# Four interleaved layers on one core: the TensorE program written out as a list of tokens, with pieces of layers 0, 1 and 2 in another order

## The chip, the cores and the metric

The kernel runs on one core of a Trainium2 chip. The time is the device time of one execution in microseconds (us); the kernel before has a median of 444.94 us over 13 runs (441.31 to 448.36). The profile shows one execution of its own, of 445.72 us. Engines are named as in the profile: PE is TensorE (PEld its weight loads), DVE VectorE, ACT ScalarE, POOL GpSimd, SP SyncE, which here only issues DMAs.

## The reference

One sequence of 2048 tokens by 512 features passes through four residual layers: a linear-attention block (A), a gated feed-forward block (B), and the same two with the same weights again. The listing is cut to what is computed.

```python
def _A_ref(x, wqkv, wo):                      # 32 heads of 16
    q, k, v = ...                             # from x @ wqkv
    phi = lambda t: jnp.where(t > 0, t + 1, jnp.exp(t)) + 1e-6
    pq, pk = phi(q), phi(k)
    kv = jnp.einsum("bhsd,bhse->bhde", pk, v)
    z = jnp.einsum("bhsd->bhd", pk)
    num = jnp.einsum("bhqd,bhde->bhqe", pq, kv)
    den = jnp.einsum("bhqd,bhd->bhq", pq, z)[..., None] + 1e-6
    return (num / den) ... @ wo
def _B_ref(x, w_gate, w_up, w_down):          # inner size 1792
    return (silu(x @ w_gate) * (x @ w_up)) @ w_down

x = x + _A_ref(_layernorm(x), A_wqkv, A_wo)   # layer 0
x = x + _B_ref(_layernorm(x), ...)            # layer 1
x = x + _A_ref(_layernorm(x), A_wqkv, A_wo)   # layer 2
x = x + _B_ref(_layernorm(x), ...)            # layer 3
```

The sums kv and z run over all 2048 tokens, so no token's attention output exists before the last key is in.

## The kernel before

**Tiles.** The tokens are 16 tiles of 128 (`T`), in 4 groups of 4 (`G`, `TG`). X, all weights and the normalised X of an attention layer (`xnA`) stay in SBUF. The 512 features are 4 chunks of 128 (`NC`), the inner size is 14 chunks (`NF`).

**Steps.** A layer's input is normalised by tile in `ln`: mean and variance (layer 0: DVE; later layers: a row sum that the residual addition leaves in `sums`, then an ACT Square with a sum), 1/sqrt on POOL (L462), then normalised on DVE (L473), or in layer 0 for 12 tiles on ACT (L469) with a factor from POOL (L466). A DMA issued on SP then transposes the tile into `xnT` (L489); only the first four tiles of layer 0 go through PE instead (L481). An attention layer then has these steps:

- `k_proj` and `q_proj`: 4 matmuls each, 128x512. `phi` follows: an exponential on ACT (L502), on about half of them an addition on ACT (L505), and minimum and maximum on DVE (L507, L511 or L514).
- `g_acc`: G = xn^T pk, summed over 16 tiles in four pinned PSUM banks; `z_acc`: the sums of keys, four 128x1 matmuls per tile.
- `z_fin`, `g_copy`, `kvt`, `m_mm`: the masked z, the copies of G, then kv and its product with Wo, which ends as `GT`.
- `den`: 16 matmuls of 128x8 give the denominators of a group of queries; DVE adds 1e-6 and takes the reciprocal (L608, L611), ACT spreads it over 16 columns (`rrep`, L616, four per group), SP issues a DMA that transposes each into `RT` (L620), and DVE multiplies the queries by it (L626).
- `wo`: 4 matmuls per tile, then DVE adds the residual (L637) and `ln` of the next layer starts for this tile.

A feed-forward layer has `gu` (gate and up of one chunk for one group: 8 matmuls, tanh on ACT L656, two DVE operations L658 and L661) and `dn` (one tile's output: 14 matmuls, residual on DVE L677).

**Order.** The order of PE's instructions is the order in which Python issues them. For the other engines `schedule` takes among the instructions that could start soonest the one whose result is due first by its own estimates; after that each engine runs its list strictly in order, and `sync` adds a semaphore wait wherever an operand comes from another engine. On PE, in layer 0, the products `gz` run two tiles behind the keys and queries of groups 0 and 1 are mixed in from tile 10. After the last `gz` come `z_fin`, `g_copy`, `den` of group 0, and so on; `wo` of groups 0 and 1 stand before the first `gu`; `weave` spreads the eight `wo` of groups 2 and 3 over the first two groups of layer 1. The keys of layer 2 for tiles 0 to 11 are mixed into layer 1's groups 1 to 3; G, z and the queries of layer 2 follow after layer 1 has ended. In layer 2 the list holds 15 of the 16 projections of queries: the first one of group 2 is in the `else` branch, which layer 2 doesn't take, and isn't issued.

**Weights.** The keys' weights come on ACT's queue at the start, X on SP's. The other weights are issued on POOL's queue, first the queries' weights (`Wq`), then the rest, in pairs tied to the keys of tile 7 and later (`load_next`).

The pieces meet in these lines of the main program:

```python
q(0, 1, 3)
gz(0, T - 1)
for L in (0, 2):
    z_fin(L)
    g_copy()
```

## Time and profile before

| what | value |
| --- | --- |
| median of 13 runs (lowest, highest) | 444.94 us (441.31, 448.36) |
| the profiled execution: its time, its span | 445.72 us, 444.0 us |
| busy in the span: PE, DVE, ACT, POOL | 420.3, 301.3, 189.9, 65.0 us |
| mean granted PE clock | 0.988 |
| DMA traffic | 24.28 MB, of which 16.27 MB on SP's queue (with the transposes) |

A row of the trace's list in order of time has the start, the time until the last of its instructions ended, the engine and the line, then the operation, its tiles and shape, the count, and in brackets how long the engine had been idle and whose result it then had. Matmuls overlap: a run of them is read from its start to the start of the next run. All `mm` calls have the one line L366, so matmuls are told apart by tiles: `pb<-pk,xnA` is G, `pb<-ones,pk` is z, `pb<-Wqkv,xnT` a key, `pb<-xnT,Wqkv` a query, `pb<-Zm,pq` a den, `pb<-GT,Wqkv` kv, `pb<-GT,pq` a `wo`, `pb<-xnT,Wg` and `pb<-xnT,Wu` gate and up, `pb<-Wd,hT` a `dn`.

### The profile page before, as it was taken

To read this page: it belongs to the slowest core of one execution; us is meant where nothing else is said; L and a number is where in the kernel's file an instruction comes from. 1 tells how busy PE (TensorE), PEld (TensorE's weight loads), DVE (VectorE), ACT (ScalarE), POOL (GpSimd) and SP (SyncE) were. 2 spreads that over 40 slices of the span, in tenths; PEclk is the share of its full clock that TensorE was granted. 3 is DMA by queue.
4 is the path that set the end of the run, shared out by engine and by line. 5 is a ranking of instruction groups with operands and counts; after the bars stand their busy time and mean duration, and the time that the engine had idled before them with its cause. 6 is when DMAs were issued, how large, how long until landed. Compare 5 with 4: busy or idle time off the path is not lost.

```text
span 444.0 us, 6441 instructions
## 1 busy us (share of the span) xinstructions
PE 420.3 (95%) x2135; PEld 192.7 (43%) x2177; DVE 301.3 (68%) x653; ACT 189.9 (43%) x361; POOL 65.0 (15%) x167
## 2 busy tenths in 40 slices
PE   6969986999999999999999997799999999999997
PEld 2434432444444444444444452344444444444443
DVE  6936878886698568738853278988758846854761
ACT  4953678444345334424432158754413402311320
POOL 4853202221211020020002000321100100000000
PEclk9999999999999999999999998999999999999999
DMA  7499543322312020011001002441130020001001
GB/s 236 78 170 337 199 96 71 60 38 47 61 36 25 3 44 1 1 25 24 1 1 38 12 1 59 84 83 37 37 83 13 13 49 24 0 13 35 1 1 47
DMA packets 56721, 24.28 MB, mean 55 GB/s; under 512 B 50736, under 2 KB 55344, under 8 KB 56688
## 3 DMA queue, kind: packets, MB, share of 16 engines
q1 hardware_dynamic: 54560, 16.27, 18.0%
q0 software_dynamic: 1584, 7.08, 4.9%
q10 hardware_dynamic: 544, 0.52, 0.4%
q8 instruction: 17, 0.28, 0.3%
q14 instruction: 16, 0.13, 0.1%
HBM read 9.70 MB, written 2.10 MB: 27 GB/s over the span
## 4 chain that ended last, share of the span: by engine, by line
PE 80%; DVE 7%; DMA 4%; POOL 3%; ACT 2%; issue 2%; SPq 1%; DVEq 0%; ACTq 0%
PE pb L366 80%; POOL rstd L462 1%; DMA Wqkv<-in_A_wqkv_dram 1%; DVE X L637 1%; SPq L620 1%; DMA xnT<-xnB 1%; DMA RT<-rrep 1%; DVE stats L445 1%; DVE pq L514 1%; ACT rrep L616 1%; DVE etmp L507 1%; DMA X<-in_A_x_dram 1%; POOL vpe L447 1%; POOL nmr L466 0%; DVE tht L658 0%
## 5 line engine op out<-in xcount | busy, mean ns | idle before, releaser
L656 ACT ACTIVATE tht<-pb 128x512 f32<-128x512 f32 x112 | 66.8, 596 | 131.1 <-PE pb L366 127.2
L366 PE MATMUL pb<-xnT,Wg 128*128 128x512 bf16 x439 | 114.9, 381 | 6.2 <-DMA xnT<-xnB 5.7
L366 PE MATMUL pb<-xnT,Wu 128*128 128x512 bf16 x438 | 114.4, 381 | 0.5
L366 PE MATMUL pb<-Wd,hT 128*128 128x512 bf16 x438 | 97.1, 379 | 0.5
L658 DVE SCALAR_TENSOR_TENSOR tht<-tht,pb 128x512 f32<-128x512 f32 x112 | 76.8, 686 | 22.6 <-ACT tht L656 19.4
L661 DVE TENSOR_TENSOR hT<-tht,pb 128x512 bf16<-128x512 f32 x112 | 76.9, 686 | 10.3 <-PE pb L366 0.5
L366 PEld LDWEIGHTS pb<-xnT,Wg 128*128 128x128 bf16 x448 | 43.9, 98 | 58.8 <-issue 6.6
L366 PEld LDWEIGHTS pb<-xnT,Wu 128*128 128x128 bf16 x448 | 44.0, 98 | 53.5 <-issue 0.9
L366 PEld LDWEIGHTS pb<-Wd,hT 128*128 128x128 bf16 x448 | 43.7, 98 | 52.4
L502 ACT ACTIVATE etmp<-pb 128x512 bf16<-128x512 f32 x63 | 37.4, 597 | 47.3 <-PE pb L366 45.5
L458 POOL TENSOR_SCALAR vpe<-mv 128x1 f32<-128x1 f32 x48 | 10.0, 209 | 266.9 <-ACT xnB L455 158.5
L366 PE MATMUL pb<-GT,pq 128*128 128x512 bf16 x127 | 33.3, 396 | 4.7 <-DVE pq L626 4.3
L462 POOL TENSOR_TENSOR rstd<-vpe,negh 128x1 f32<-128x1 f32 x64 | 36.7, 574 | 6.3
L366 PE MATMUL pb<-xnT,Wqkv 128*128 128x512 bf16 x118 | 30.1, 382 | 3.7 <-DMA Wqkv<-in_A_wqkv_dram 3.3
L507 DVE TENSOR_SCALAR etmp<-etmp 128x512 bf16<-128x512 bf16 x63 | 18.2, 291 | 22.2 <-ACT etmp L502 21.3
L366 PE MATMUL pb<-Wqkv,xnT 128*128 128x512 bf16 x123 | 32.7, 384 | 0.5 <-issue 0.2
L366 PE MATMUL pb<-pk,xnA 128*128 128x512 bf16 x127 | 32.7, 383 | 0.1
L677 DVE SCALAR_TENSOR_TENSOR pq<-pb,X 128x512 bf16<-128x512 f32 x16 | 11.1, 692 | 30.7 <-PE pb L366 30.7
L455 ACT ACTIVATE xnB<-X,mv 128x512 bf16<-128x512 bf16 x32 | 23.0, 721 | 11.7 <-DVE mv L452 10.5
L473 DVE TENSOR_SCALAR xnA<-X,mv,rstd 128x512 bf16<-128x512 bf16 x20 | 8.2, 411 | 26.1 <-POOL rstd L462 26.1
L455 ACT ACTIVATE xnA<-X,mv 128x512 bf16<-128x512 bf16 x16 | 11.5, 722 | 33.4 <-DVE mv L452 33.4
L637 DVE SCALAR_TENSOR_TENSOR X<-pb,X 128x512 bf16<-128x512 f32 x32 | 21.9, 683 | 1.9 <-PE pb L366 1.9
(62 smaller groups left out, 284.8 us busy)
## 6 DMA issues: line engine op xcount, KB each, us to landing
out_dram<-pq SPq DMA_DIRECT2D x16, 128.0 KB, 1.7
Wu<-in_B_w_up_dram POOLq DMA_DIRECT2D x4, 448.0 KB, 6.0
Wg<-in_B_w_gate_dram POOLq DMA_DIRECT2D x4, 448.0 KB, 6.4
X<-in_A_x_dram SPq DMA_DIRECT2D x6, 256.0 KB, 5.3
Wd<-in_B_w_down_dram POOLq DMA_DIRECT2D x3, 512.0 KB, 5.0
Wqkv<-in_A_wqkv_dram POOLq DMA_DIRECT2D x2, 512.0 KB, 5.9
X<-in_A_x_dram SPq DMA_DIRECT2D x4, 128.0 KB, 3.4
Wqkv<-in_A_wqkv_dram ACTq DMA_DIRECT2D x2, 256.0 KB, 3.5
```

The source lines that it names most:

```text
L366: return op("pe", lambda e: e.matmul(o_ap, lhsT=lhsT, rhs=rhs, start=start, stop=stop, skip_group_check=skip), r=r, w=w, occ=occ, lat=occ ...
L455: op("act", lambda a: a.activation(out=b_ap, in_=X[:, t, :], func=ACT.Square, bias=mv[:, t, 0:1], accum_out=mv[:, t, 1:2]), r=[xk, f"mv{t} ...
L458: op("pool", lambda p: p.tensor_scalar(out=vpe[:, t:t + 1], in0=mv[:, t, 1:2], scalar1=1.0 / D, scalar2=1e-5, op0=ALU.mult, op1=ALU.add), ...
L462: op("pool", lambda p: p.tensor_tensor(out=rstd[:, t:t + 1], in0=vpe[:, t:t + 1], in1=negh[:], op=ALU.pow), r=[f"vp{t}", "negh"], w=[f"rs{ ...
L473: op("dve", lambda v: v.tensor_scalar(out=b_ap, in0=X[:, t, :], scalar1=mean, scalar2=rstd[:, t:t + 1], op0=sub, op1=ALU.mult), r=[xk, f"m ...
L502: op("act", lambda a: a.activation(out=etmp[e][:], in_=PB[pb][:], func=ACT.Exp), r=[f"pb{pb}"], w=[f"e{e}"], occ=0.485, lat=0.6)
L507: op("dve", lambda v: v.tensor_scalar(out=etmp[e][:], in0=etmp[e][:], scalar1=1.0, scalar2=1e-6, op0=ALU.min, op1=ALU.add), r=[f"e{e}"], w ...
L637: op("dve", lambda v: v.scalar_tensor_tensor(out=X[:, t, :], in0=PB[pb][:], scalar=1.0, in1=X[:, t, :], op0=ALU.mult, op1=ALU.add, accum_o ...
L656: op("act", lambda e: e.activation(out=tht[a][:], in_=PB[pg][:], func=ACT.Tanh, scale=0.5), r=[f"pb{pg}"], w=[f"th{a}"], occ=0.485, lat=0.6)
L658: op("dve", lambda v: v.scalar_tensor_tensor(out=tht[a][:], in0=tht[a][:], scalar=1.0, in1=PB[pg][:], op0=ALU.add, op1=ALU.mult), r=[f"pb{ ...
L661: op("dve", lambda v: v.tensor_tensor(out=hT[h][:, j, :], in0=tht[a][:], in1=PB[pu][:], op=ALU.mult), r=[f"pb{pu}", f"th{a}"], w=[f"h{h}_{ ...
L677: op("dve", lambda v: v.scalar_tensor_tensor(out=o_ap, in0=PB[pb][:], scalar=0.5, in1=X[:, t, :], op0=ALU.mult, op1=ALU.add, **kw), r=[f"p ...
```

## The change

PE's program is now a string, PROGRAM. A token is a layer, a letter and indices: `t` a transposition on PE, `k` keys of a tile, `q` queries (group, chunk), `g` and `z` the sums, `d` a quarter of a den (group, chunk), `v` kv, `m` a quarter of its product with Wo, `w` a `wo` tile, `u` gate and up (group, chunk), `n` a `dn` tile, `S` a warming matmul. A second list, ON_ACT, fixes what goes to ACT instead of DVE. With that:

- `z` runs ahead of `g` in both attention layers; the dens of groups 0 to 2 now stand among the last `g` and the queries, ahead of `v`; the den of group 3 stands between `w7` and `w8`.
- `w0` to `w11` stand in a row before layer 1 (and 3); only `w12` to `w15` are mixed with the first group's gate and up.
- Eight projections of queries of layer 2 (groups 0 and 1) are mixed into layer 1's groups 2 and 3, beside the keys, which move by some places. All 16 are issued.
- `Wq` is loaded on SP's queue behind X. All other weights stay on POOL's queue, in one run that waits until the last transposition of layer 0's input has landed.
- In layer 0, DVE normalises 12 of the 16 tiles and ACT 4 (before: 4 and 12). Eight of its 16 keys take the addition on ACT (before: five).
- The negated mean of layers 1 to 3 moves from DVE to POOL; the Square reads `sums` itself. The reciprocals are stored as bf16.
- The very last `dn` tile is computed in two halves of 256 columns, each with its own residual and its own output DMA.

```diff
+PROGRAM = """
+S S S S S S S S S S S 0t0 S S 0t1 0k0 0t2 0k1 0t3 0k2 0g0 0z0 0k3 0g1 0z1 0k4 0g2 0z2 0k5 0g3 0z3 0k6 0g4 0z4
+0k7 0g5 0z5 0k8 0g6 0z6 0k9 0g7 0z7 0k10 0g8 0z8 0k11 0z9 0k12 0g9 0z10 0q00 0k13 0g10 0q01 0k14 0q02 0k15
+0q03 0q10 0z11 0z12 0z13 0z14 0q11 0z15 0q12 0d00 0d01 0d02 0d03 0g11 0q13 0g12 0q20 0d10 0d11 0d12 0d13 0q21
+0g13 0q22 0g14 0q23 0g15 0d20 0d21 0d22 0d23 0q30 0q31 0v 0q32 0m0 0m1 0m2 0m3 0q33 0w0 0w1 0w2 0w3 0w4 0w5
+0w6 0w7 0d30 0d31 0d32 0d33 0w8 0w9 0w10 0w11 1u000 1u001 1u002 0w12 1u003 1u004 0w13 1u005 1u006 0w14 1u007
+1u008 0w15 1u009 1u010 1u011 1u012 1u013 1n0 1n1 1n2 1n3 1u100 1u101 1u102 1u103 1u104 1u105 1u106 2k0 1u107
+1u108 2k1 1u109 1u110 1u111 2k2 1u112 1u113 2k3 1n4 1n5 1n6 1n7 1u200 1u201 1u202 1u203 1u204 2q00 1u205 2q01
+1u206 1u207 2q02 1u208 2q03 1u209 2k4 1u210 1u211 2k5 1u212 2k6 1u213 2k7 1n8 1n9 1n10 1n11 1u300 1u301 1u302
+1u303 1u304 2q10 1u305 2q11 1u306 1u307 2q12 1u308 2q13 1u309 2k8 1u310 1u311 2k9 1u312 2k10 1u313 2k11 1n12
+1n13 1n14 1n15 2z0 2z1 2z2 2z3 2z4 2z5 2z6 2z7 2z8 2z9 2z10 2z11 2q20 2q21 2q22 2q23 2g0 2g1 2g2 2k12 2g3 2k13
+2g4 2k14 2g5 2k15 2g6 2z12 2z13 2z14 2g7 2z15 2d00 2d01 2d02 2d03 2g8 2q30 2g9 2d10 2d11 2d12 2d13 2g10 2q31
+2g11 2d20 2d21 2d22 2d23 2g12 2g13 2g14 2g15 2q32 2v 2q33 2m0 2m1 2m2 2m3 2w0 2w1 2w2 2w3 2w4 2w5 2w6 2w7 2d30
+2d31 2d32 2d33 2w8 2w9 2w10 2w11 3u000 3u001 3u002 2w12 3u003 3u004 2w13 3u005 3u006 2w14 3u007 3u008 2w15
+3u009 3u010 3u011 3u012 3u013 3n0 3n1 3n2 3n3 3u100 3u101 3u102 3u103 3u104 3u105 3u106 3u107 3u108 3u109
+3u110 3u111 3u112 3u113 3n4 3n5 3n6 3n7 3u200 3u201 3u202 3u203 3u204 3u205 3u206 3u207 3u208 3u209 3u210
+3u211 3u212 3u213 3n8 3n9 3n10 3n11 3u300 3u301 3u302 3u303 3u304 3u305 3u306 3u307 3u308 3u309 3u310 3u311
+3u312 3u313 3n12 3n13 3n14 3n15
+"""
...
+ON_ACT = set("""
+0k1 0k3 0k5 0k7 0k9 0k11 0k13 0k15 0q01 0q03 0q11 0q13 0q21 0q23 0q31 0q33 0G0 0G2 0M0 0M2 2k1 2k3 2k5 2k7 2k9
+2k11 2k13 2k15 2q01 2q03 2q11 2q13 2q21 2q23 2q31 2q33 2G0 2G2 2M0 2M2 0t0 0t1 0t2 0t3 0x5 0x8 0x11 0x14
+""".split())
...
-        weights.append(lambda a: dma("pool", Wqkv[:, :, 0:D], wq3[:, :, 0:D], 512, w=["Wq"], after=a, occ=1.0))
+        dma("sp", Wqkv[:, :, 0:D], wq3[:, :, 0:D], 512, w=["Wq"], prio=-80)
         weights.append(lambda a: dma("pool", Wqkv[:, :, 2 * D:], wq3[:, :, 2 * D:], 512, w=["Wv"], after=a,
                                      occ=1.0))
...
             if L == 0:
-                op("dve", lambda v: v.bn_stats(stats[:, t, :], X[:, t, :]), r=[xk], w=[f"st{t}"], occ=0.6)
-                op("dve", lambda v: v.bn_aggr(mv[:, t, :], stats[:, t, :]), r=[f"st{t}"], w=[f"mv{t}"], occ=0.1)
-                op("pool", lambda p: p.tensor_scalar(out=vpe[:, t:t + 1], in0=mv[:, t, 1:2], scalar1=1e-5,
-                                                     scalar2=None, op0=ALU.add),
-                   r=[f"mv{t}"], w=[f"vp{t}"], occ=0.2, lat=0.25)
+                op("dve", lambda v: v.bn_stats(stats[:, t, :], X[:, t, :]), r=[xk], w=[f"st{t}"], occ=0.6,
+                   kind="stats")
+                op("dve", lambda v: v.bn_aggr(mv[:, t, :], stats[:, t, :]), r=[f"st{t}"], w=[f"mv{t}"], occ=0.075,
+                   lat=0.2, kind="aggr")
                 mean, sub = mv[:, t, 0:1], ALU.subtract
-            else:
-                op("dve", lambda v: v.tensor_scalar(out=mv[:, t, 0:1], in0=sums[:, t:t + 1], scalar1=-1.0 / D,
-                                                    scalar2=None, op0=ALU.mult),
-                   r=[f"sm{t}"], w=[f"mv{t}"], occ=0.07, lat=0.14)
-                op("act", lambda a: a.activation(out=b_ap, in_=X[:, t, :], func=ACT.Square,
-                                                 bias=mv[:, t, 0:1], accum_out=mv[:, t, 1:2]),
-                   r=[xk, f"mv{t}"], w=[bk, f"ss{t}"], occ=0.62, lat=0.75)
-                op("pool", lambda p: p.tensor_scalar(out=vpe[:, t:t + 1], in0=mv[:, t, 1:2], scalar1=1.0 / D,
-                                                     scalar2=1e-5, op0=ALU.mult, op1=ALU.add),
-                   r=[f"ss{t}"], w=[f"vp{t}"], occ=0.2, lat=0.25)
+                var, scale, vk = mv[:, t, 1:2], 1.0, f"mv{t}"
+            else:
+                op("act", lambda a: a.activation(out=b_ap, in_=X[:, t, :], func=ACT.Square, scale=-float(D),
+                                                 bias=sums[:, t:t + 1], accum_out=mv[:, t, 1:2]),
+                   r=[xk, f"sm{t}"], w=[bk, f"ss{t}"], occ=0.71, lat=0.8, kind="sq")
+                op("pool", lambda p: p.tensor_scalar(out=mv[:, t, 0:1], in0=sums[:, t:t + 1], scalar1=-1.0 / D,
+                                                     scalar2=None, op0=ALU.mult),
+                   r=[f"sm{t}"], w=[f"mv{t}"], occ=0.18, lat=0.25, kind="negm")
                 mean, sub = mv[:, t, 0:1], ALU.add
+                var, scale, vk = mv[:, t, 1:2], 1.0 / D ** 3, f"ss{t}"
+            op("pool", lambda p: p.tensor_scalar(out=vpe[:, t:t + 1], in0=var, scalar1=scale, scalar2=1e-5,
+                                                 op0=ALU.mult, op1=ALU.add),
...
+            if f"{L}x{t}" in ON_ACT:
...
-                   r=[xk, f"nm{t}", f"rs{t}"], w=[bk], occ=0.705, lat=0.81)
+                   r=[xk, f"nm{t}", f"rs{t}"], w=[bk], occ=0.705, lat=0.77, kind="apply")
             else:
                 op("dve", lambda v: v.tensor_scalar(out=b_ap, in0=X[:, t, :], scalar1=mean,
                                                     scalar2=rstd[:, t:t + 1], op0=sub, op1=ALU.mult),
-                   r=[xk, f"mv{t}", f"rs{t}"], w=[bk], occ=0.325, lat=0.4)
+                   r=[xk, f"mv{t}", f"rs{t}"], w=[bk], occ=0.325, lat=0.4, kind="apply")
...
+            if not gb:
+                gb.extend([bank(pin=True) for _ in range(NC)] + [0])
             for c in range(NC):
-                mm(gb[c], xnA[:, t, c * P:(c + 1) * P], pk[t][:], t == 0, t == T - 1,
+                mm(gb[c], xnA[:, t, c * P:(c + 1) * P], pk[t][:], gb[NC] == 0, gb[NC] == T - 1,
                    r=[f"xa{t}", f"pk{t}"], w=[f"pb{gb[c]}"])
+            gb[NC] += 1
+            if gb[NC] == T:
+                for c in range(NC):
+                    evac(gb[c], GT[:, c, :], f"GT{c}", f"{L}G{c}")
+                    pinned.discard(gb[c])
+                gb.clear()
 
...
+        def z_acc(L, t):
             if L not in zb:
-                zb[L] = bank(pin=True)
...
+            for c in range(NC):
+                mm(pb, pk[t][:, c * P:(c + 1) * P], ones[:], n == 0 and c == 0, n == T - 1,
+                   r=[f"pk{t}", "ones"], w=[f"pb{pb}"], occ=MM1, cols=(c, c + 1), skip=True)
+            if n == T - 1:
+                op("dve", lambda v: v.tensor_tensor(
+                    out=Zm[:], in0=PB[pb][:, 0:NC].unsqueeze(2).to_broadcast([P, NC, HC]),
+                    in1=mask[:, 0:P:DH].unsqueeze(1).to_broadcast([P, NC, HC]), op=ALU.mult),
+                   r=[f"pb{pb}", "mask"], w=["Zm"], occ=0.1, lat=0.17, kind="zm")
+                pinned.discard(pb)
...
+        def den(L, g, j):
+            if (L, g) not in db:
+                db[L, g] = bank(pin=True), r_den.take(TG if f"{L}d{g}" in PE_T else 0), set()
+            pb, d, seen = db[L, g]
+            b = pq_of[L, g]
+            for tl in range(TG):
+                mm(pb, pq[b][:, j, tl * P:(tl + 1) * P], Zm[:, j, :], True, True,
+                   r=[f"pq{b}_{j}_{tl}", "Zm"], w=[f"pb{pb}"], occ=MM1,
+                   cols=(tl * H + HC * j, tl * H + HC * (j + 1)), skip=True)
+            seen.add(j)
+            if len(seen) < NC:
+                return
+            pinned.discard(pb)
...
-               r=[f"pb{pb}"], w=[f"dsb{d}"], occ=0.22, lat=0.3)
+               r=[f"pb{pb}"], w=[f"dsb{d}"], occ=0.2, lat=0.32, kind="den")
             op("dve", lambda v: v.reciprocal(out=rtok[d][:], in_=dsb[d][:]), r=[f"dsb{d}"], w=[f"rtok{d}"],
-               occ=0.87, lat=0.96)
-            R = r_RT.take()
+               occ=0.87, lat=0.95, kind="den")
...
-                                                       op0=ALU.mult, op1=ALU.add, **kw),
-               r=[f"pb{pb}", f"x{t}"], w=ok + ([f"sm{t}"] if L < 3 else []), occ=0.607, lat=0.72)
+            last = L == 3 and len(ended) == T
+            ended.add(t if L == 3 else -1)
+            for lo, hi in ((0, D // 2), (D // 2, D)) if last else ((0, D),):
+                pb = bank()
+                for j in range(NF):
+                    mm(pb, hT[h][:, j, tl * P:(tl + 1) * P], Wd[:, j, lo:hi], j == 0, j == NF - 1,
+                       r=[f"h{h}_{j}", f"Wd{j}"], w=[f"pb{pb}"], occ=MM * (hi - lo) / D, cols=(0, hi - lo))
+                kw = dict(accum_out=sums[:, t:t + 1]) if L < 3 else {}
+                hk = ok if L < 3 else ok[lo * TG // D:hi * TG // D]
+                op("dve", lambda v, pb=pb, lo=lo, hi=hi: v.scalar_tensor_tensor(
+                    out=o_ap[:, lo:hi], in0=PB[pb][:, 0:hi - lo], scalar=0.5, in1=X[:, t, lo:hi],
+                    op0=ALU.mult, op1=ALU.add, **kw),
+                   r=[f"pb{pb}", f"x{t}"], w=hk + ([f"sm{t}"] if L < 3 else []),
+                   occ=0.607 * (hi - lo) / D, lat=0.72 * (hi - lo) / D, kind="res")
+                if L == 3:
+                    dma("sp", out2d[t * P:(t + 1) * P, lo:hi], o_ap[:, lo:hi], 128 * (hi - lo) // D, r=hk)
...
+        late_consts([o for o in pr.ops if o.kind == "pow"][:TG])
+        last = [o for o in pr.ops if o.kind == "xT"][-1:]
+        for w_ in weights:
+            w_(last)
```

## The prediction

> **What bounds the kernel now.** The page first: PE is busy 95% of the span, DVE 68%. PE's steady pace is read in layer 1, and every departure from it is lost time. In the list in order of time, 56 matmuls of a `dn` group take 199.15 - 187.07 = 12.08 us, 0.2157 each:
>
> ```profile
> 187.07 12.25 PE L366 MATMUL pb<-Wd,hT 128*128 128x512 bf16 x55
> 199.15 1.03 PE L366 MATMUL pb<-xnT,Wg 128*128 128x512 bf16 x4
> ```
>
> At that pace the program's matmuls cost: 1,873 of 512 columns (13 of them warming) 404.0 us; 48 of 128 columns 2.7 (kv: 16 from 52.47 to 53.36); 256 of 1 or 8 columns 6.7 (den: 16 from 269.02 to 269.43). Sum 413.4. So 444.0 - 413.4 = 30.6 us of the span is not work, and the list says where. Before the first matmul 1.2, then 4.3 in the start up to the first z at 12.65; 3.4 after the last matmul at 440.6. The other 21.6 are three places, the same that PE's waits name:
>
> ```profile
> PE pb L366 <- DMA xnT<-xnB: 5.7, 2, 3.3
> PE pb L366 <- DVE pq L626: 4.3, 5, 2.6
> PE pb L366 <- DMA Wqkv<-in_A_wqkv_dram: 3.3, 1, 3.3
> ```
>
> (B) the wait for `Wq`: from 27.37 to 35.18 PE does 2.7 us of work, 5.1 lost:
>
> ```profile
> 27.27 0.24 PE L366 MATMUL pb<-ones,pk 128*128 128x1 bf16 x4
> 30.81 1.44 PE L366 MATMUL pb<-xnT,Wqkv 128*128 128x512 bf16 x4 [3.30 <-DMA Wqkv<-in_A_wqkv_dram]
> ```
>
> (C) layer 0's den and `wo`, 50.46 to 79.61: 16.9 us of work end at the first gate at 74.47, 7.1 lost, and 1.7 more because the next matmuls run slowly (16 take 5.1 us instead of 3.5):
>
> ```profile
> 70.61 0.55 PE L366 MATMUL pb<-Zm,pq 128*128 128x8 bf16 x16
> 74.47 1.02 PE L366 MATMUL pb<-xnT,Wg 128*128 128x512 bf16 x4 [3.32 <-DMA xnT<-xnB]
> ```
>
> (E) the same stretch of layer 2, 264.6 to 288.28, 7.7 lost: 0.5 for kv's mask, 2.8 at `w0` plus 1.7 of slow matmuls, 0.2, and 2.5 at the first gate:
>
> ```profile
> 269.43 1.02 PE L366 MATMUL pb<-xnT,Wqkv 128*128 128x512 bf16 x4
> 273.06 5.30 PE L366 MATMUL pb<-GT,pq 128*128 128x512 bf16 x16 [2.61 <-DVE pq L626]
> 285.37 0.55 PE L366 MATMUL pb<-Zm,pq 128*128 128x8 bf16 x16
> 288.28 1.02 PE L366 MATMUL pb<-xnT,Wg 128*128 128x512 bf16 x4 [2.36 <-DMA xnT<-xnB]
> ```
>
> Between these places PE has no gap, so the change can win at most 21.6 us and what it saves at the ends.
>
> **The change, part by part.**
>
> *Work.* Layer 2's missing query projection is now issued: 4 matmuls, +0.9. The half-width matmuls have the same columns: 0.
>
> *Wq on SP's queue.* X's last bytes come at 10.0 in the second-by-second stretches (253 GB/s in 9 to 10, 11 in 10 to 11). 0.52 MB at 340 GB/s add 1.5, done by 11.5; SP's first transposition is issued at 11.92. So the queue that Wq is put into is empty in time, and it is there 20 us before its first use. B's 5.1 goes, slow matmuls included. What is late next there: keys. Per tile DVE now does statistics 0.59, aggregate 0.09, normalisation 0.33, minimum 0.2, maximum 0.61 or 0.33: mean 1.68 against PE's 1.83 for k, g and z. Thin, but covered; if it isn't, each 0.1 costs 1.6. POOL loses 8 factors of 0.29.
>
> *Start and tail.* The first four tiles are as before: 0. The last residual is half as long: 0.69 to 0.36, -0.3.
>
> *den early, C.* Gaps between a result and its user, in PE's new order, one 4-matmul step being 0.86. Keys and queries need 2.3 us from their last matmul to the end of phi (the key of 25.55 leaves PE at 26.4, its maximum ends at 28.7). z15 has three steps of cover behind the last key, then Zm: 0.5 for queueing. `d1` has two steps behind its last query, and three quarters of its own 0.42: 0.3. `d2` has one step: 1.1. kv and `m` have one to two steps where before one: 0.3. `w0` behind `m`, with one query between, waits for the copies of GT: 0.5. First gate: `w3`'s tile must pass DVE, ACT, POOL and a transposition. DVE's list from `w0`'s residual to the fourth normalisation holds eight residuals (0.68 with the sum), five multiplications, four normalisations, two maxima (0.335) and a minimum: 9.4; it begins 1.0 after `w0` starts, the transposition takes 2.45, together 12.9; PE covers twelve `wo` and a den, 10.8: 2.1. Bounds of this one: 0, if ACT and POOL run well beside it, and 4.4, from 11.7 us between `w3` and the gate in the old list less 7.3 of cover; I take the walk along the queue, which is this program's own. C together 4.8 instead of 8.8.
>
> *den early, its transpositions.* They were issued from 54.32 on, behind the weights, whose traffic ended at 52.6. Now the first den starts near 41, so its RT comes 3.0 later, near 44 to 46 (51.32 to 54.32 before). The weights now wait for tile 15's transposition, issued at 27.77 before, landing near 30; 6.55 MB at the 339 GB/s below last until about 51. On POOL nothing but weights is queued behind that wait until layer 1's input near 60, and their first user, kv, is due near 52. So the first five or six RT run beside weights. The rows for that, landing times of transpositions in 26.3 to 27.7 (beside Wq and Wo) and in 54 to 56 (alone), and the traffic (stretch, length, PE busy, clock, DMA share, GB/s):
>
> ```profile
> DMA to landing us min/median/max: 5.7/6.3/7.0
> ```
> ```profile
> DMA to landing us min/median/max: 2.4/2.4/2.4
> ```
> ```profile
> 24.00:31.00 7.00, 3.70 (x25) 1.00 1.08 197
> 35.00:44.00 9.00, 8.95 (x57) 1.00 0.96 339
> ```
>
> So they land 3.7 late. DVE's first multiplication by RT then blocks DVE, and behind it stand the maxima of group 2's queries, which `d2` and the PSUM banks wait for. Bounds: 0 (weights gone, or DVE elsewhere) and 3.7 + 1.7, if PE stops long enough to slow down. I take 3.0, near the lateness itself.
>
> The Trainium skill speaks against this overlap (DMA: Bandwidth & Descriptors, Queues, rings and completion order): each DMA engine takes turns between queues, packet by packet. Halving the transposition's share would make 2.4 into 4.8 and my 3.0 into some 2, an estimate from that page; the measured 6.3 is worse.
>
> *den early, E.* No weights move then. `d0` behind key 15's phi: 0.5. kv and mask: 0.6. `w0` directly behind `m3`, without cover for the copies of GT (0.6 on ACT, 0.68 on DVE, two each): 1.3. Gate: DVE's list is eight residuals and nine short operations, 8.5, so 1.0 + 8.5 + 2.45 - 10.8 = 1.1 (upper bound 10.1 - 7.3 = 2.8, from the old list). Together 3.5 instead of 7.7. None of these waits reaches the 2.6 us after which matmuls ran slowly, while 2.36 at 288.28 had no such effect.
>
> The skill's page TensorE: Matmul & The Clock Gate (Why this matters for your kernels) allows gaps up to about 3 us; the 2.61 gap here was enough, so the row decides. For the waits above both give nothing.
>
> *Moves that cost nothing.* Layer 2's queries inside layer 1: a group has 43 us of PE; DVE has there 17 us of L658 and L661, four residuals and normalisations, and now four keys and four queries, 26 to 28 in all. `w12` to `w15` in one group: DVE 17 + 2.7 + 1.3 + 4 = 25 of 27.6 us, covered by 8 PSUM banks; DVE was 7.8 of 8 us busy at 80 to 88 without a loss. If this cover went, the excess would be paid in full. The negated means on POOL make 1.0 us per tile, against 0.86 per `wo` but 3.0 per `dn`; only four tiles count for the gate. SP's fourth group of RT passes ahead of twelve transpositions of layer 1's input: their users are a group away.
>
> **Sum.** 1.2 + 4.3 + 414.3 + 4.8 + 3.0 + 3.5 + (3.4 - 0.3) = 434.2 of span, 9.8 under 444.0. Its execution took 445.7, so 435.9; that execution lies 0.8 above the median of the runs shown, so against the median 435.1, and I say 435.
>
> **Rivals.**
>
> 1. *No collision.* The weights start earlier or DVE has slack: the 3.0 goes, 432; the walks along queues may be pessimistic by another 2. For: 339 GB/s unshared. Against: RT starts before 51 by my count.
> 2. *Collision plus slow clock.* PE stops over 2.6 us at `d2` and at the gate, 1.7 each, and transpositions come at 1.6 instead of 1.3 us under load (the four issued from 25.1 on landed at about that pace): +5, 440. For: the slow stretches after 3.3 us waits in B and C.
> 3. *Other side.* RT is served only when the weights are through. In 24 to 31, with four transpositions in them, traffic was 197 GB/s; were the weights to run at that pace to the end, they would last till 64 instead of 51, RT's twelve transpositions would end near 80, and the gate would come 12 us later: 447. It decides from a mean below about 230 GB/s. Against: 35 to 44 shows 339.
> 4. *The move does nothing:* every wait comes back as another on the same DVE queue, 444 to 446. Against: C's and E's losses are waits with PE work in hand that the new order puts there.
>
> **Chances.** Forecast 0.58, rival 1 0.20, rival 2 0.15, rival 3 0.05, rival 4 0.02. The likeliest case's own range is 433.5 to 437.5; with rivals 1 and 2 it is 430 to 441.5, which leaves out about 0.15. A measurement of this kernel can tell about 0.3% (1.3 us): faster 0.93, same 0.02, slower 0.05.
>
> **What would show it.** Right: no wait on Wqkv near 30, `pb<-Zm,pq` in the forties, PE's waits under 3 us with L626's multiplication and xnT as releasers, PEclk without a dip outside the start, landing of RT<-rrep up to 6 us, span near 434. Wrong: RT landing above 8 us or a PE gap over 3 us before the first gate (slower than said), or RT at 2.4 (faster); DVE at 8 of 8 us with PE gaps in layer 1 group 0 or among the first keys would break the covers.

## The result and the profile after

The changed kernel takes **448.5 us** (median of 11 runs, 447.15 to 449.66) against 445.0 for the kernel before (48 runs): ratio 1.0082, 95% interval 1.0060 to 1.0104. It is slower by 0.8%, where 435 was forecast. Two further executions of it on record, of 443.95 and 450.03 us, are not among the 11. The profiled execution took 447.71 us, its span is 446.0.

The page of the kernel after: granted clock and traffic in 40 slices of 11.15 us, and the lines of the chain that ended last.

```profile
PEclk9999959899999999999999999999999999999999
...
GB/s 281 73 79 376 205 98 67 75 61 71 25 36 1 1 35 13 0 2 35 12 1 1 48 1 72 96 71 72 69 38 13 0 26 24 1 13 35 1 0 47
...
PE pb L380 83%; DMA RT<-rrep 3%; POOL rstd L472 1%; DMA xnT<-xnB 1%; SPq L651 1%; DVE X L682 1%; ACT etmp L525 1%; DVE stats L454 1%; DMA X<-in_A_x_dram 1%; POOL vpe L469 0%; ACT pq L528 0%; ACT rrep L647 0%; POOL mv L464 0%; DVE xnB L483 0%; DVE xnA L483 0%
```

The clock dips in the sixth and eighth slice (56 to 67 and 78 to 89 us), and the transposition of 1/den, RT, now stands on the chain. PE's waits in the kernel after (what it waited for, us in total, times, longest):

```profile
PE pb L380 <- DVE pq L534: 9.7, 2, 4.9
PE pb L380 <- DMA xnT<-xnB: 4.9, 2, 2.8
...
PE pb L380 <- DVE pq L537: 0.7, 1, 0.7
```

The wait for `Wqkv` is gone, as forecast. In its place the waits for the maxima of phi (L534, L537) cost 10.4 us. PE's list in order of time, kernel after, shows where:

```profile
50.71 0.24 PE L380 MATMUL pb<-Zm,pq 128*128 128x8 bf16 x4
55.81 0.27 PE L380 MATMUL pb<-Zm,pq 128*128 128x8 bf16 x4 [4.86 <-DVE pq L534]
56.81 0.27 PE L380 MATMUL pb<-Zm,pq 128*128 128x8 bf16 x4 [0.73 <-DVE pq L537]
61.88 0.27 PE L380 MATMUL pb<-Zm,pq 128*128 128x8 bf16 x4 [4.80 <-DVE pq L534]
62.01 3.57 PE L380 MATMUL pb<-xnT,Wqkv 128*128 128x512 bf16 x8
65.37 1.91 PE L380 MATMUL pb<-GT,Wqkv 128*128 128x128 bf16 x16
...
83.80 1.02 PE L380 MATMUL pb<-xnT,Wg 128*128 128x512 bf16 x4 [2.84 <-DMA xnT<-xnB]
...
267.19 0.54 PE L380 MATMUL pb<-Zm,pq 128*128 128x8 bf16 x16 [0.39 <-DVE Zm L577]
...
294.74 1.02 PE L380 MATMUL pb<-xnT,Wg 128*128 128x512 bf16 x4 [2.04 <-DMA xnT<-xnB]
```

Up to the first quarter of `d2` at 50.71 all is as said (first den at 41.27, RT from 45.4). Then `d2` (den of group 2) waits 10.4 us for the last three quarters of its queries, the eight queries behind it take 3.36 us instead of 1.73, kv 2.14 instead of 0.90, and the first gate (layer 1's first matmul) comes at 83.80. Layer 2 (267 to 295) has none of this: much the same order, and no weights in flight.

The traffic beside it (kernel after; stretch, length, then busy us and instructions of PE, PEld, DVE, ACT and POOL, the clock, DMA share, GB/s):

```profile
40.00:44.00 4.00, 4.00 (x37) 1.93 (x36) 3.54 (x10) 2.00 (x4) 1.43 (x3) 1.00 1.02 395
44.00:48.00 4.00, 3.93 (x33) 2.06 (x33) 3.08 (x8) 4.00 (x9) 2.27 (x3) 1.00 0.80 296
48.00:52.00 4.00, 2.95 (x18) 1.33 (x16) 0.09 (x1) 0.94 (x2) 0.71 (x1) 1.00 1.33 224
52.00:56.00 4.00, 0.19 (x4) 0.18 (x4) 0.96 (x3) 0.63 (x1) 0.00 (x0) 0.77 0.91 122
56.00:60.00 4.00, 0.35 (x8) 0.18 (x4) 1.30 (x3) 0.55 (x2) 0.00 (x0) 0.50 1.18 122
```

RT is issued from 45.42 on. From there all traffic falls from 395 to 122 GB/s with the DMA engines still busy (shares of 0.91 to 1.33 from 48 on); the weights alone move 1.56 MB in 40 to 44, 0.40 in 52 to 56 and 0.27 in 56 to 60, where SP's queue, with RT alone in it, holds 0.81 of the engines' time. From 48 to 60 DVE and ACT, too, do little: 2.4 and 2.1 of 12 us. RT's landing times (from issue until the data is there) in the kernel after, of those in the queue in 45 to 46, 46 to 48 (the first one again) and 48 to 50 us; these are four transpositions, issued at 45.4, 46.7, 48.0 and 49.7:

```profile
DMA to landing us min/median/max: 9.5/9.5/9.5
...
DMA to landing us min/median/max: 9.5/11.1/12.7
...
DMA to landing us min/median/max: 11.3/11.9/12.6
```

DVE's list in order of time, kernel after:

```profile
47.80 0.28 DVE L530 TENSOR_SCALAR etmp<-etmp 128x512 bf16<-128x512 bf16 x1
54.99 0.42 DVE L660 TENSOR_TENSOR pq<-pq,RT 128x512 bf16<-128x512 bf16 x1 [6.91 <-DMA RT<-rrep]
55.34 0.42 DVE L534 TENSOR_TENSOR pq<-pq,etmp 128x512 bf16<-128x512 bf16 x1
...
59.39 0.42 DVE L660 TENSOR_TENSOR pq<-pq,RT 128x512 bf16<-128x512 bf16 x1 [2.64 <-DMA RT<-rrep]
...
61.41 0.41 DVE L534 TENSOR_TENSOR pq<-pq,etmp 128x512 bf16<-128x512 bf16 x1
```

ACT's list of the same stretch:

```profile
48.32 0.62 ACT L525 ACTIVATE etmp<-pb 128x512 bf16<-128x512 f32 x1
55.08 0.63 ACT L647 ACTIVATE rrep<-rtok 128x512 bf16<-128x512 bf16 x1 [6.13 <-DMA RT<-rrep]
59.45 0.63 ACT L647 ACTIVATE rrep<-rtok 128x512 bf16<-128x512 bf16 x1 [3.74 <-DMA RT<-rrep]
59.98 0.58 ACT L525 ACTIVATE etmp<-pb 128x512 bf16<-128x512 f32 x1
60.46 0.68 ACT L528 ACTIVATE pq<-pb,onep 128x512 bf16<-128x512 f32 x1
```

Both engines stand still for the same late transpositions. DVE's multiplication L660 reads RT; ACT's copy L647 waits to overwrite one of four `rrep` buffers that a transposition has not yet read. Behind them, in strict order, stand the maximum (L534) and the exponential (L525) that `d2` needs.

By the way of the forecast, 446.0 - 414.3 of work = 31.7 us are lost, where 19.9 were said:

| place | said | lost |
| --- | --- | --- |
| start, up to the first z (12.60) | 5.5 | 5.5 |
| B, wait for `Wq` | 0 | 0 |
| C with the collision, 12.60 to 88.93 | 4.8 + 3.0 | 19.5 |
| E, 251.24 to 294.74 (39.6 of work) | 3.5 | 3.9 |
| tail, from 443.43 | 3.1 | 2.6 |
| elsewhere | 0 | 0.2 |

C's 19.5 are 10.4 at `d2`, 2.8 of slow matmuls behind it, 2.84 at the gate, 1.7 of slow matmuls behind that, and 1.8 in pieces below 0.8.

### The profile page after: what moved, and what is told of

It reads as the page before. It is cut to its first block, busy times and chain, and to the rows that moved or that the text cites. A ratio compares the mean times of both kernels' runs of the same rounds, so it can differ in the third digit from the quotient of the medians.

```text
span 446.0 us, 6428 instructions
## 1 busy us (share of the span) xinstructions
PE 421.8 (95%) x2154; PEld 195.6 (44%) x2195; DVE 300.0 (67%) x618; ACT 185.2 (42%) x353; POOL 72.9 (16%) x206
## 3 DMA queue, kind: packets, MB, share of 16 engines
q0 software_dynamic: 1440, 6.55, 5.1%
## 4 chain that ended last, share of the span: by engine, by line
PE 83%; DMA 5%; DVE 4%; ACT 2%; POOL 2%; issue 2%; SPq 1%; DVEq 0%; ACTq 0%
PE pb L380 83%; DMA RT<-rrep 3%; POOL rstd L472 1%; DMA xnT<-xnB 1%; SPq L651 1%; DVE X L682 1%; ACT etmp L525 1%; DVE stats L454 1%; DMA X<-in_A_x_dram 1%; POOL vpe L469 0%; ACT pq L528 0%; ACT rrep L647 0%; POOL mv L464 0%; DVE xnB L483 0%; DVE xnA L483 0%
## 5 line engine op out<-in xcount | busy, mean ns | idle before, releaser
L380 PE MATMUL pb<-Wd,hT 128*128 128x512 bf16 (+1 forms) x454 | 97.6, 372 | 0.4
L707 DVE TENSOR_TENSOR hT<-tht,pb 128x512 bf16<-128x512 f32 x112 | 76.8, 686 | 9.4
L380 PEld LDWEIGHTS pb<-Wd,hT 128*128 128x128 bf16 x462 | 45.2, 98 | 51.7 <-DVE hT L707 0.2
L525 ACT ACTIVATE etmp<-pb 128x512 bf16<-128x512 f32 x64 | 37.4, 594 | 22.8 <-PE pb L380 19.5
L464 POOL TENSOR_SCALAR mv<-sums 128x1 f32<-128x1 f32 x48 | 11.7, 246 | 190.1 <-DVE X L730 114.6
L380 PE MATMUL pb<-xnT,Wqkv 128*128 128x512 bf16 x123 | 32.8, 396 | 1.0 <-DVE pk L537 0.5
L730 DVE SCALAR_TENSOR_TENSOR pq<-pb,X 128x512 bf16<-128x512 f32 (+1 forms) x17 | 11.2, 660 | 33.3 <-PE pb L380 33.3
L483 DVE TENSOR_SCALAR xnA<-X,mv,rstd 128x512 bf16<-128x512 bf16 x28 | 11.5, 411 | 28.2 <-POOL rstd L472 25.6
L380 PE MATMUL pb<-GT,pq 128*128 128x512 bf16 x124 | 29.4, 379 | 0.7 <-DVE GT L588 0.2
L461 ACT ACTIVATE xnB<-X,sums 128x512 bf16<-128x512 bf16 x32 | 23.0, 719 | 15.1 <-DMA xnT<-xnB 8.4
L647 ACT ACTIVATE rrep<-rtok 128x512 bf16<-128x512 bf16 x32 | 18.8, 629 | 16.6 <-DMA RT<-rrep 10.8
L461 ACT ACTIVATE xnA<-X,sums 128x512 bf16<-128x512 bf16 x16 | 11.5, 720 | 31.9 <-DVE X L730 31.9
```

Source lines behind the costliest of these rows:

```text
L380: return op("pe", lambda e: e.matmul(o_ap, lhsT=lhsT, rhs=rhs, start=start, stop=stop, skip_group_check=skip), r=r, w=w, occ=occ, lat=occ ...
L461: op("act", lambda a: a.activation(out=b_ap, in_=X[:, t, :], func=ACT.Square, scale=-float(D), bias=sums[:, t:t + 1], accum_out=mv[:, t, 1 ...
L464: op("pool", lambda p: p.tensor_scalar(out=mv[:, t, 0:1], in0=sums[:, t:t + 1], scalar1=-1.0 / D, scalar2=None, op0=ALU.mult), r=[f"sm{t}" ...
L483: op("dve", lambda v: v.tensor_scalar(out=b_ap, in0=X[:, t, :], scalar1=mean, scalar2=rstd[:, t:t + 1], op0=sub, op1=ALU.mult), r=[xk, f"m ...
L525: op("act", lambda a: a.activation(out=etmp[e][:], in_=PB[pb][:], func=ACT.Exp), r=[f"pb{pb}"], w=[f"e{e}"], occ=0.48, lat=0.55, kind="exp")
L647: op("act", lambda a, tl=tl, q=q: a.activation(out=rrep[q][:].rearrange("p (h j) -> p h j", j=DH), in_=rtok[d][:, tl * H:(tl + 1) * H].uns ...
```

## The experiments

Two theories at first. **Collision**: the weights, not the order, cost the 10 us. **Order**: DVE and ACT are too full for a den ahead of G, and late RT is only a part of it. Each kernel is told by its edit against the changed kernel, and each time with its ratio to the kernel before in the same runs (the changed kernel's is 1.0082). The expectations say 6.0 MB for POOL's loads; the page has 6.55.

### Is it the weights?

**wd_late**, the last quarter of the weights moved away:

```diff
-        for w_ in weights:
+        for w_ in weights[:-4]:
             w_(last)
...
+            if tok == "1u002":
+                last = [o for o in pr.ops if o.kind == "rT"][-1:]
+                for w_ in weights[-4:]:
+                    w_(last)
```

> The only edit: the four loads of Wd (1.8 MB of the 6.0 MB that POOL still loads) are issued after the last RT transposition of layer 0 instead of directly behind Wu; the order of PE, DVE and ACT up to the first gate stays. Theory 1 (the RT transpositions of the first dens share the DMA engines with the weights, come 9.5 to 12.7 us after their issue, and block DVE): without Wd the weights end near 44, RT is issued from 45.4 on and lands in 2.4 us, the two stops of 4.9 and 4.8 us at d2 and the slow matmuls behind them go, the first gate comes at 71 to 73 instead of 83.8, and the time is 436 to 438 us. Theory 2 (the order itself: DVE's and ACT's queues are too full for a den ahead of G, and the transpositions are only the last in line): the gaps stay, 446 to 449. Theory 3 (the weights are late as such): kv or the first gate then wait for weights, and the time is 447 or more.

440.07 us, ratio 0.9897 (0.9858 to 0.9935). RT's landing times from 40 to 66 us in wd_late:

```profile
DMA to landing us min/median/max: 2.4/2.5/4.1
```

PE's list in wd_late:

```profile
52.66 0.26 PE L380 MATMUL pb<-Zm,pq 128*128 128x8 bf16 x4 [1.20 <-DVE pq L534]
...
58.18 1.02 PE L380 MATMUL pb<-Wo,KVT 128*128 128x512 bf16 x4 [1.76 <-DVE KVT L598]
...
73.37 1.03 PE L380 MATMUL pb<-xnT,Wg 128*128 128x512 bf16 x4 [2.55 <-DMA xnT<-xnB]
```

The stops at `d2` shrink from 10.4 to 1.2 us, the forecast's 1.1, and the gate comes 10.4 us sooner. Collision is shown; theory 2 in its strong form falls. But 440 is not 436 to 438.

**wd_half**, `weights[:-2]` and `weights[-2:]` in the same places:

> Between the changed kernel and wd_late: two of the four loads of Wd stay directly behind Wu (1.05 MB), two come after RT. If the lateness is the time the weights still need when RT is issued, they are through about 3 us sooner than in the changed kernel at least (1.05 of 1.8 MB of traffic beside RT): stops at d2 of 3 to 7 us in all instead of 10.4, time 441 to 445. If any weight beside RT costs the whole stop, 446 to 448; if only the last loads matter, 439.5 to 441.

441.96 us, 0.9923 (0.9893 to 0.9953). The three RT issued from 46.2 to 48.9 land in 4.2 to 5.9 us, the stops are 1.24 + 0.74 + 1.81 = 3.8. The lateness goes with the bytes still on their way: none of Wd, 2.4 to 4.1 us (wd_late); two loads of Wd, 4.2 to 5.9; all four, 9.5 to 12.7.

**w_early4**, `[-1:]` of the last transposition replaced by `[-4:-3]`:

> One edit: the weights on POOL wait for the transposition of tile 12 instead of tile 15's, issued 3 to 5 us earlier. Theory 1: they end 3 to 5 us sooner, less lateness of RT: the two stops at d2 shrink from 9.7 to 3 to 6 us, time 441 to 445; the three transpositions of tiles 13 to 15 land 3 to 5 us later, and if the keys have no slack for that, 1 to 3 us come back between 27 and 37. Theory 2: no change at d2, 447 to 450.

442.07 us, 0.9920 (0.9883 to 0.9957), from 439.0 to 445.8 in ten runs. In its profiled execution (439.03, the fastest of the ten) the stops are 0.74 + 1.81. Starting the weights sooner helps as much as holding half of Wd back, and the keys did have the slack.

**rt_pe**, the transposition taken off the DMA queues instead, with tokens `0r00` to `0r23`, each four PE transposes, behind the dens:

```diff
-PE_T = set("0t0 0t1 0t2 0t3".split())
+PE_T = set("0t0 0t1 0t2 0t3 0d0 0d1 0d2".split())
...
+                op("pe", lambda e, c=c: e.transpose(out=tp[:, c * P:(c + 1) * P],
+                                                    in_=rrep[q][:, c * P:(c + 1) * P], identity=ident[:]),
```

> The weights are loaded as in the changed kernel; the first three dens of layer 0 send 1/den through PE instead of the DMA engines: ACT's rrep stays, then four 128-column transposes into PSUM per tile (48 in all, +2.7 us of PE) and the multiplication reads PSUM; group 3's RT and layer 2 stay on the DMA queue. Theory 1 (collision): with no RT beside them the weights run on at 380 to 400 GB/s and end near 48, no stop above 2 us before the gate, no slow matmuls there; 446.0 - 10.4 (the stops) - 1.5 to 3 (slow matmuls) + 2.7 + 2 to 3 of new short waits for rrep: time 437 to 442. Theory 2 (DVE and ACT are too full for a den ahead of G): DVE has more to do here, the stops at d2 stay near 5 us, time 449 or more.

440.81 us, 0.9887 (0.9840 to 0.9934), within the range of theory 1. All weights stay where they were, and traffic drops to 40 GB/s in 52 to 56; the longest stop ahead of the gate is 0.8 us, the gate's own 1.43.

### By which way does late RT stop PE?

**rrep12**: twelve buffers, so ACT never waits for RT.

```diff
+                if L == 0 and g < 3:
+                    rr, rk = hT[0][:, 4 * g + tl, :], f"h0_{4 * g + tl}"
+                else:
+                    q = r_rrep.take()
+                    rr, rk = rrep[q][:], f"rrep{q}"
```

> The weights as in the changed kernel, so RT still lands 9 to 13 us late; but the copies of 1/den (rrep) of the first three dens have twelve buffers instead of four (they lie in hT[0], unused until the first gate), so that ACT never waits for a late transposition to read its buffer. If ACT's wait is what makes the second long stop (its exp of the last query quarter stood behind rrep until 59.45): that stop shrinks from 4.8 to 2 or less, 444 to 446. If DVE's own order is enough (its second RT multiplication, released at 59.4, stands ahead of that quarter's maximum): 1 us at most is won, 446.5 to 448.5.

**no_scale**: DVE never waits for RT. The kernel leaves out the multiplication, so layer 0's attention is not divided by den in groups 0 to 2 and DVE has less to do.

```diff
+                if L or g == 3:
                     scale(L, g, tl, RT[R][:, :, tl * P:(tl + 1) * P], f"RT{R}_{tl}", 0.335)
```

> Leaves out the twelve multiplications of q by RT of groups 0 to 2 of layer 0 (so layer 0's attention is not divided by den there); RT is still made and transposed, four rrep buffers as before. DVE no longer waits for RT at all and has 5 us less to do; ACT still waits for its rrep buffers. If DVE's queue alone were the way by which late RT stops PE, both stops go: 434 to 438. If ACT's queue does it as well, the exp of the last query quarter still comes at 60 and PE stops for as long in one piece: 444 to 448.

**rrep12_no_scale**: both.

> Both of the former two at once (the twelve multiplications left out, twelve buffers for rrep), the weights and the transpositions beside them as in the changed kernel. RT is as late as ever but nobody waits for it: no stop above 2 us before the first gate, 433 to 438. If there is a stop of 4 us or more at d2 here, lateness of RT is not the cause.

446.78 us (1.0057, 1.0030 to 1.0083), 445.41 (1.0006, 0.9979 to 1.0032) and 440.30 (0.9905, 0.9872 to 0.9939). The long waits in PE's list of rrep12:

```profile
57.44 0.27 PE L380 MATMUL pb<-Zm,pq 128*128 128x8 bf16 x4 [6.13 <-DVE pq L534]
...
61.58 0.27 PE L380 MATMUL pb<-Zm,pq 128*128 128x8 bf16 x4 [2.88 <-DVE pq L534]
```

the longest one of no_scale:

```profile
61.71 0.27 PE L380 MATMUL pb<-Zm,pq 128*128 128x8 bf16 x4 [10.10 <-DVE pq L534]
```

and of rrep12_no_scale:

```profile
75.81 1.87 PE L380 MATMUL pb<-xnT,Wg 128*128 128x512 bf16 x4 [6.74 <-DMA xnT<-xnB]
```

SP's list in rrep12_no_scale has the cause of the last one:

```profile
68.22 6.22 SPq L492 DMA_TRANSPOSE xnT<-xnB  x4
```

With DVE freed, ACT alone holds the last maximum until 61.7: one stop of 10.1 instead of three that sum to 10.4. With ACT freed, DVE alone stops PE for 6.13 + 0.73 + 2.88 = 9.7. Only both together open `d2` (1.2 us), and then the lateness comes out at a third place, which I had not expected: SP works off twelve RT transpositions until 68.2, issues layer 1's first one only then, and the gate waits 6.74; the time, 440.3, misses the 433 to 438 said. Three queues in order carry the same delay. By the ratios, ACT freed is worth 1.1 us (the intervals overlap), DVE freed 3.4, both 7.9, of which a part is the 5 us of work that DVE no longer has.

### What is left of C without a collision

The first attempt at the old order: **den_late0**, PROGRAM of layer 0 with `g` beside `z` again and the dens behind G:

```diff
-0q03 0q10 0z11 0z12 0z13 0z14 0q11 0z15 0q12 0d00 0d01 0d02 0d03 0g11 0q13 0g12 0q20 0d10 0d11 0d12 0d13 0q21
...
+0q03 0q10 0g11 0z11 0g12 0z12 0q11 0g13 0z13 0q12 0g14 0z14 0q13 0g15 0z15 0q20 0d00 0d01 0d02 0d03 0v 0q21 0m0 0m1 0m2 0m3 0q22
+0d10 0d11 0d12 0d13 0q23 0w0 0w1 0w2 0w3 0q30 0w4 0w5 0q31 0w6 0w7 0q32 0q33 0d20 0d21 0d22 0d23 0d30
```

> Undoes one part: in layer 0 alone the dens and the order of G, kv, m and wo are the old ones (den 0 behind G, den 1 behind m, den 2 behind all queries); layers 1 to 3, the load of Wq and everything else as in the changed kernel. Theory 1 (collision): the weights end near 48, RT of den 0 is issued near 51, no collision; C costs about its old 8.8, B and E stay won: 444.0 - 5.1 - 4.2 + 0.9 - 0.3 = 435.3 of span, time 436 to 439. Theory 3 (the loads of the weights, which now begin at 31.25, are what costs, wherever the den stands): 445 or more. If the gains of B or E were not real, it would also stay at 441 or more.

443.37 us, 0.9962 (0.9938 to 0.9985). That is in the last range (441 or more), which would make the gains of B or E unreal; but the edit was not what its expectation says: `d3` and `w8` to `w11` had stayed ahead of the first gate, so `w8` waits 3.20 us directly behind `d2`. It tells nothing of the old order.

**l0_old** puts them behind the first gates too (`w8` to `w11` after `1u002`, `1u004`, `1u006`, `1u009`, `d3` after `1u011`, `w12` to `w15` in the next group); **l0_old_wd** is the same with wd_late's edit.

> Undoes the layer-0 half of the change, now with the old places of w8 to w15 and den 3 too (behind the first gates); Wq on SP, layer 2 and the rest as changed. den 0 comes near 50, RT from 51 on; den_late0 showed weights still moving until about 56 beside it. If theory 1 holds and the late start of the weights (they move from 33.5 on, 24 to 28 before) matters even here, C is 8.8 plus 1 to 3: 438 to 441. If it does not matter, 436 to 438. If B's or E's gain were not real, 442 or more.

> As l0_old, and Wd loaded late as in wd_late, so neither order has weights beside RT. Compared with wd_late (440.1) it gives the worth of den ahead of G by itself. By my walk along the queues the old order loses 4.0 more in C: 444. If the walk was wrong and C is bound by DVE in both orders, they are within 1.5: 438.5 to 441.5, and the new order in layer 0 is worth nothing.

438.36 us (0.9836, 0.9787 to 0.9885) and 438.84 (0.9834, 0.9772 to 0.9895). The first lies at the low end of its 438 to 441, the second in 438.5 to 441.5. Two answers: undoing the order in layer 0 alone is worth 10 to 11 us to the changed kernel, and with no weights beside RT in either order the new one (wd_late, 440.1) is not faster than the old; the intervals overlap. My 4.0 for it is refuted.

**wd_d2_late** and **wd_d2_no_scale**: wd_late with a looser order (`0q30 0v 0q31 0d20 0d21 0d22 0d23 0m0 0m1 0m2 0m3 0q32 0w0 0w1 0w2 0w3 0q33 0w4`), the second also with no_scale's edit.

> wd_late (no weights beside RT) with PE's order before the first gate loosened: d2 three steps later, v before q31, q32 and q33 among w0 to w7. It removes the 1.2 us at d2 and the 1.8 at the kv mask. If C's remaining loss is a matter of PE's order, the time falls by 2 to 3: 437 to 438. If DVE's work (24.1 us of the 28 between 48 and 76 in wd_late) sets it, the wait comes back at the first gate (2.55 there, 4 to 5 here): 439 to 441.

> wd_d2_late with the twelve multiplications by RT of groups 0 to 2 of layer 0 left out (its output is not divided by den there): 5.0 us less of DVE between 48 and 66, no weights beside RT, PE's order the loosened one. If DVE's work is what sets the rest of C's loss, the stop at the first gate goes from 4.1 to 1.5 or less, with the slow matmuls behind it, and the time from 438.6 to 433 to 436. If the chain through ACT, POOL and the transposition sets the gate, the stop stays at 3.5 to 4.5 and the time at 438 to 440.

438.61 us (0.9863, 0.9823 to 0.9904) and 440.44 (0.9874, 0.9831 to 0.9916, runs from 436.8 to 443.3). The first: PE runs without a gap of 0.3 us from 38 to 68, then waits 4.09 at the gate, where it was 2.55 (its profiled execution, 440.96, is the slowest of four); the waits moved on, and the time lies between the two ranges. The second has another fault: in its profiled execution Wd, now issued at 81.4, meets layer 1's transpositions, ACT's Square waits 10.74 us for xnT, tanh stands behind it, and PE stops 5.90 us at 97. So Wd had been moved into the next collision; the 1.5 us that wd_late loses in its first down group (`hT` L707, waits that the changed kernel lacks) fit that.

**wd_clean** and **wd_clean_no_scale** keep Wd clear of all transpositions: wd_d2_late up to `w11`, then `1u000` to `1u013` alone, `d3`, and `w12` to `w15` in the next group; Wd waits for tile 11's transposition.

> Dens ahead of G with no weights beside any transposition: the loosened order of wd_d2_late up to w11; den 3 and w12 to w15 go behind layer 1's first group, where they were in the kernel before, and Wd is issued after the transposition of tile 11, into a stretch of gate and up alone. The stops of 1.3 to 1.5 us in the first down group of wd_late and wd_d2_late (Wd beside xnT) go. If DVE's work sets C, the stop at the gate stays at 4 to 5 and the time is 437 to 438.5, no better than the old order's 438.4; if it falls to 435 or less, dens ahead of G were right and only Wd's place was wrong.

> The same with the twelve multiplications by RT of groups 0 to 2 of layer 0 left out (no division by den there), 5.0 us less of DVE. wd_d2_no_scale could not tell, since a stop of 5.9 us came with Wd in layer 1; its gate stop was 2.3. Here: if DVE's work sets C, the gate stop is 1.5 to 3 and the time 2 to 4 us below wd_clean's. If the chain behind DVE does, the two are within 1 us.

438.09 us (0.9835, 0.9803 to 0.9867) and 436.20 (0.9786, 0.9756 to 0.9817). The stretch from 48 to 72 in wd_clean (columns as above):

```profile
48.00:72.00 24.00, 19.96 (x118) 9.38 (x115) 23.18 (x65) 17.05 (x36) 7.65 (x24) 1.00 0.48 84
```

and in wd_clean_no_scale:

```profile
48.00:72.00 24.00, 20.87 (x120) 9.82 (x119) 19.59 (x52) 17.68 (x38) 8.04 (x26) 0.97 0.49 88
```

The gate in PE's list of wd_clean:

```profile
72.07 1.86 PE L381 MATMUL pb<-xnT,Wg 128*128 128x512 bf16 x4 [4.00 <-DMA xnT<-xnB]
```

and of wd_clean_no_scale:

```profile
70.80 1.86 PE L381 MATMUL pb<-xnT,Wg 128*128 128x512 bf16 x4 [3.13 <-DVE xnB L484]
```

In wd_clean DVE is busy 23.2 of 24 us and PE waits 4.00 at the gate: DVE is full there. With 3.6 us less on DVE the stop is still 3.13 and the time 1.9 lower by the medians, 2.2 by the ratios, whose intervals overlap: at the edge of the 2 to 4 that were to mark DVE's work. The time is a poor witness here: of the 2.7 us between the two profiled spans, 1.7 are slow matmuls behind layer 3's first gate, which only wd_clean's execution has. The gate itself comes 1.3 earlier. So DVE's work is likely a part of it; how the remaining 3.1 divide between its order and the chain through ACT, POOL and the transposition stays open.

C's loss with no collision, by PE's list: in wd_clean the first z is at 12.65 and the gate at 72.07, with 53.0 us of work between (56 steps of 0.863 for keys, G, queries and `wo`, 4.7 of `m`, kv and the small matmuls), so 6.4 are lost, and 1.6 to slow matmuls behind the gate: 8.0. In wd_late, whose order is that of the changed kernel, with one den more, it is 12.39 to 73.37, 60.98 - 53.43 = 7.55, and 1.69 to slow matmuls: 9.2. In l0_old the gate is at 70.39, with four `wo` less: 57.7 - 49.6 = 8.1, and no slow matmuls:

```profile
70.39 1.02 PE L381 MATMUL pb<-xnT,Wg 128*128 128x512 bf16 x4 [2.26 <-DMA xnT<-xnB]
```

In l0_old_wd it is 8.0 and 1.4: 9.4. All are near the 8.8 of the kernel before.

### The two other parts alone

**before_wq_sp**, on the kernel before:

```diff
-        weights.append(lambda a: dma("pool", Wqkv[:, :, 0:D], wq3[:, :, 0:D], 512, w=["Wq"], after=a, occ=1.0))
+        dma("sp", Wqkv[:, :, 0:D], wq3[:, :, 0:D], 512, w=["Wq"], prio=-80)
```

> One part alone, on the kernel before: Wq is loaded on SP's queue behind X instead of on POOL's. If stage B's 5.1 us is the wait for Wq and nothing else, the time goes from 445 to 440 (439 to 441), and the weights on POOL end earlier by the same 0.5 MB. If the keys' phi chain on DVE is nearly as late as Wq was, 442 to 444.

441.42 us, 0.9917 (0.9888 to 0.9947): 3.9 us less by the medians, 4.5 by the spans, a little under the 5.1 and just above the range of 439 to 441. The wait for `Wq` is gone and nothing takes its place before C.

**l2_old**, the changed kernel with layer 2's tokens in the old order (queries behind the last key, dens behind G, `w8` to `w15` behind the gates; here all 16 query projections are issued):

> Undoes the other part: the changed kernel with layer 2 (its queries, dens, G, kv, m and wo, and layer 3's mixing) in the old order, with layer 0 as changed. If the step E was sized rightly (7.7 of loss before, 3.5 now), the time is 4.2 longer than the changed kernel's: 452 to 453.5. If the queries inside layer 1 cost there what they save in layer 2, it is the same, 447.5 to 449.5.

450.56 us, 1.0117 (1.0068 to 1.0165): 0.35% or 1.6 us above the changed kernel by the ratios, 2.7 by the spans, with intervals that overlap. The gain is smaller than the 4.2 said, the time between the two ranges; and of the 2.7, 1.7 are slow matmuls behind layer 3's first gate (a gap of 2.39), which the changed kernel's execution doesn't have. The stop of 2.61 at `w0` that the kernel before has does not come back here (0.29 + 0.51 instead), so part of E's gain seems to come with the fixed shares of ACT and DVE, not with the order; no run took these alone.

## Why the prediction was wrong

- **B, Wq on SP's queue: right.** No wait, no slow matmuls; the part alone is worth 3.9 to 4.5.
- **Start, tail, layer 2's extra projection: right** within 0.5.
- **E: right in the whole** (3.9 lost against 3.5), but not term by term: the gate's wait is 2.04, where 1.1 was said, and the rest 1.9, where 2.4 was. The total is also luck: in seven other traces a gap as long was followed by slow matmuls, 1.7 more. The gain over the old order is smaller than the 4.2 said (l2_old).
- **"den early, its transpositions": right mechanism, wrong size; this step failed.** C lost 19.5 us with the collision and, in the same order, 9.2 without (wd_late), so its price is 10.3, where 3.0 was said and 5.4 was the upper bound; against wd_clean's looser order (8.0) it is 11.5. Three things were too small. The landing: 9.5 to 12.7 us instead of 6.3, a figure read from transpositions that met two loads, while these met up to four. The ways: only DVE's queue was followed, and ACT's `rrep` buffers and SP's own order carry the same delay. The consequence: slow matmuls, 2.8 at `d2` and 1.7 at the gate, were put into rival 2 at 1.7 each.
- **Rival 3 came nearest**, at 0.05. It said that RT is served when the weights are through, the gate 12 us later, 447, and that it decides from a mean below 230 GB/s. Three of the first four RT landed from 59.4 to 61.0, within about 1 us of the last weight at 60.4; the first landed at 54.9, before it. The gate came 10 us later than the forecast's sum puts it. The 6.55 MB took from 31.25 (first issue) to 60.4 (the last one, issued at 48.10, landed 12.3 later): 225 GB/s. The 339 GB/s that spoke against it was measured where no transposition was in flight. That is an error behind the size: the weights' pace was taken from a stretch without RT, to decide how long RT would have to run beside them.
- **"den early, C": wrong.** 4.8 was said; with the collision away, the orders tried lose 8.0 to 9.4. The walk let DVE begin its list 1.0 us after `w0` with nothing before it; in wd_clean DVE is busy from before `w0` (56.69) to the gate without a pause above 0.23 us. The gate's term was 2.1; it is 2.55 in wd_late and 4.0 in wd_clean, plus 1.7 and 1.6 of slow matmuls. kv and `m` were 0.3; in wd_late the wait for kv's mask alone is 1.76. The first keys were "thin, but covered"; 0.5 to 0.6 twice were not.
- **Slow matmuls "after 2.6 us": not a length.** The forecast gave 1.7 to no wait because 2.61 had cost it and 2.36 had not. The last section shows that the place of these two gaps, and not their length, was the difference.
- **What it would take to see it beforehand:** each in-order queue that issues, overwrites or reads RT is a place where its lateness can be paid. There are three.

The sum: of the 11.8 us between the forecast span and the measured one, 7.3 are the collision, 4.4 C itself, 0.1 the rest (with wd_clean for wd_late, 8.5, 3.2 and 0.1).

The Trainium skill (DMA: Bandwidth & Descriptors, Queues, rings and completion order) was cited for turns packet by packet, from which 4.8 us was estimated; the runs show 9.5 to 12.7. The same section states two things that I had passed over: a turn is a whole packet of many descriptors, and a completion mark lands only after every earlier write of its DMA engine, across the queues. Both would make a transposition wait longer beside weights than equal shares do; no run here tells them apart.

The fastest versions that leave nothing out are wd_clean (438.1 us, 0.9835), l0_old (438.4, 0.9836) and l0_old_wd (438.8, 0.9834): the change with a looser order and the weights kept clear of the transpositions, or with its order in layer 0 undone. They are not told apart. About half of their gain is the load of `Wq`, which alone has 0.9917.

## What to carry to other kernels

When a step is moved earlier, ask which transfers it will now share the DMA engines with, and take the pace of both from a stretch in which both run; here 339 and 395 GB/s of weights alone became 122 of both together. A late transfer can be paid in every in-order queue that reads, refills or follows its buffer, and opening one of them showed the next. If bulk loads are not needed yet, hold them until the small transposes are done, and check that the new place is not the next collision.
